# Multi-query attention beside a spectral filter: every fold of the first Fourier stage on VectorE, its constant as 128 rows, and a reordered end of the opening stage

## The chip, the cores and the metric

The kernel runs on one core of one Trainium2 chip. The metric is the device time in microseconds. Three runs of the kernel before the change took 697.56, 697.57 and 697.76 us; the median is 697.57 us. One more execution was profiled: it took 697.94 us, and its first to its last instruction span 696.1 us. All times inside the kernel below are microseconds from the start of that span.

## The reference

Two independent parts work on two inputs of 2048 rows by 448 columns, and their results are put side by side.

Part A is attention with 16 heads of width 28 that share one key and one value head:

```
q = (x @ wq) as 16 heads;  k = x @ wk;  v = x @ wv
p = softmax(q @ k.T * 28 ** -0.5)
a = concat(p @ v) @ wo
```

Part B is a global filter in the frequency domain:

```
X = rfft2(x);  X = X * (w_r + 1j * w_i);  b = irfft2(X)
```

All inputs and the result are float32.

## The kernel before

The kernel has an opening stage (up to about 97 us) and an attention stage (from there to the end).

In the opening stage the projections are computed and the forward transform of part B along the 448 columns and the first step along the 2048 rows are done. The projection x times wq runs in four chunks c of 512 rows and four groups g of four heads; each group holds a few spare rows in which k and v travel along. A float32 operand is split into a rounded high part and a rest (`split_w`, `split_x`), and one group of one chunk is eleven products (line 267) into one PSUM bank `pq`. ScalarE copies the bank to `qraw` (line 271, in `evac`) and VectorE takes the largest absolute value of it (line 272, `qmx`). The four groups of chunk 0 come first; the loop from line 310 then runs the twelve pairs (c, g) with c from 1 to 3, counted by n = 4(c-1)+g from 0 to 11.

The transform's first stage comes in eight portions q. For each portion, `fft1_load` brings a 512 KB block `xb` and a small table `fw` on SyncE's DMA queue, with four `xb` buffers in all. `fft1_fold` forms the sums and differences that the symmetry of the transform allows, into a tile `f` of two buffers, so that fold q+2 has to wait for the products that read fold q. `fft1_a` multiplies `f` by the constant `cs1` (64 products, line 120) and `fft1_b` multiplies the result by `fw` (16 products, line 132); then two stores per portion put the result into a DRAM tile `t1` (line 142). The tuple `slots` names the pairs n after which a portion's `fft1_a`, the load of portion q+4, the fold of portion q+2 and `fft1_b` of portion q-1 stand.

A fold is eight tensor-tensor operations: two of 113x512 at line 99 (one sum, one difference), two more of 113x512 at lines 102 and 103, and four of 113x256 at lines 104 to 107. Before the change the differences of lines 99 and 103 run on GpSimd (POOL), the rest on VectorE (DVE).

The keys and values are gathered out of the spare rows of `qraw` into the tile `kf` by small transfers (`fetch`, line 197): fourteen on SyncE's queue, seven on GpSimd's. `keys` splits the keys into `ka`. `kf` is first filled with a column of constants, `cvk`, by a GpSimd copy (line 291). 

At the end of the stage comes a bound on the scores. `qmx` is reduced to `qm`, multiplied to `prod` (line 355), a product with `blk` (line 357) gives `cvec`, four small products (line 363) and a reduction give one number `bits` (line 364). Each engine loads `bits` into a register (line 368) and branches (line 369): if the bound is too large, a slow path corrects the queries; the data here do not take it. `build_q(0, 0, True)` makes the first group's query tile `qa` with DVE and ScalarE copies; it stands before the computation of `bits`. After the branch the values are transposed by sixteen products (line 401) and copied to `vs` (line 402).

The attention stage has 256 half steps: two products `s` (line 649), an exponential on ScalarE (line 652) and, one step later, the products with the values (line 631). The second and third stages of the transform are put between these by a list written out in the code (`at`, `mid`).

TensorE's (PE) instructions run in the order of the program (line 181). For the other engines and the queues the framework's scheduler sets the order, by its own estimates; each engine then executes its list strictly in order, waiting on semaphores. SyncE's queue (SP) and GpSimd's issue their DMAs in order too, so that one that has to wait holds up those behind it. `behind` gives the scheduler an order of issue and adds no semaphore.

The PSUM pool `p1` has eight banks in the opening stage; the attention pools `ps_x`, `ps_s` and `ps_o` are opened after it has been closed.

Of the kernel before, what the change touches and what calls it, by code (L numbers as in the profile page):

```python
# [9 lines left out]
F32 = mybir.dt.float32  # L10
# [4 lines left out]
ALU = mybir.AluOpType  # L15
# [23 lines left out]
def kernel(ctx: ExitStack, tc: tile.TileContext, t: dict):  # L39
# [41 lines left out]
    def fft1_consts():  # L81
        fc["cs1"] = fp.tile([113, 4, 113], F32, name="cs1", tag="cs", bufs=1)
        nc.sync.dma_start(fc["cs1"], t["cs1"])
# [10 lines left out]
    def fft1_fold(q):  # L94
        x = xb[q][0][:113]
        f = ff[q] = fp.tile([113, 4, 4, 2, 32], F32, name="f", tag="wi")
        xv = x.rearrange("p k (j h m) -> p k j h m", h=2, m=32)
        for h, (eng, op) in enumerate(((nc.vector, ALU.add), (nc.gpsimd, ALU.subtract))):
            eng.tensor_tensor(f[:, :, :, h], xv[:, :, :, 0], xv[:, :, :, 1], op=op)
# [3 lines left out]
        nc.gpsimd.tensor_tensor(o2, y[:, 0::2], y[:, 1::2], op=ALU.subtract)  # L103
        nc.vector.tensor_tensor(y[:, 0], e2[:, 0], e2[:, 1], op=ALU.add)
        nc.vector.tensor_tensor(y[:, 1], e2[:, 0], e2[:, 1], op=ALU.subtract)
        nc.vector.tensor_tensor(y[:, 2], o2[:, 0], o2[:, 1], op=ALU.subtract)
        nc.vector.tensor_tensor(y[:, 3], o2[:, 0], o2[:, 1], op=ALU.add)
# [3 lines left out]
    def fft1_a(q):  # L111
        f, cs1 = ff.pop(q), fc["cs1"]
        for p in range(2):
            pa = ps1[0].tile([128, 2, DF], F32, name="pa", tag="p")
            for e in range(2):
                for k, (n, o0) in enumerate(((113, 0), (112, 113))):
                    for h in range(2):
                        for r in range(2):
                            r0 = 64 * h + 32 * r
                            mm(pa[r0:r0 + 32, e, o0:o0 + n], f[:, 2 * r + k, 2 * p + e, h], cs1[:, 2 * r + k, :n],  # L120
                               start=True, stop=True)
            a = at1[q, p] = fp.tile([128, 2, DF], F32, name="a", tag=("pwr", "pwi")[p])
            nc.scalar.activation(a, pa, AF.Copy)  # L123

    def fft1_b(q):
        w = xb[q][1]
        pb = [ps1[0].tile([128, 2, DF], F32, name="pbb", tag="p") for _ in range(2)]
        for p in range(2):
            a = at1.pop((q, p))
            for h in range(2):  # L130
                for e in range(2):
                    mm(pb[h][64 * e:64 * e + 64, p], w[64 * h:64 * h + 64, 2 * p + e], a[64 * h:64 * h + 64, e],
                       start=True, stop=True)
        bs = fp.tile([128, 2, 2, DF], F32, name="bs", tag="cst" if q < 6 else "b2")
        for h in range(2):
            if q < 7:
                nc.scalar.activation(bs[:, h], pb[h], AF.Copy)
            else:
                nc.vector.tensor_copy(bs[:, h], pb[h])
        for e in range(2):  # L140
            n0 = 16 * e + 2 * q
            nc.sync.dma_start(t1.rearrange("(l s) n f -> s l n f", l=2)[:, :, n0:n0 + 2], bs[64 * e:64 * e + 64])

    def fft2_consts():
        for n in ("g1", "g2"):
            g = fp.tile([128, 128], F32, name=n, tag="g", bufs=1)
            nc.sync.dma_start(g, t[n])
            h = fc[n + "h"] = fp.tile([128, 128], F32R, name=n + "h", bufs=1)
# [6 lines left out]
    def build_q(c, g, first=False):  # L155
# [10 lines left out]
        for u in range(2):  # L166
# [9 lines left out]
            if first:  # L176
                nc.vector.tensor_copy(q[64:128, 2 * u:2 * u + 2], q[0:64, 2 * u:2 * u + 2].bitcast(F32))
        if not first:
            nc.sync.dma_start(q[64:128].bitcast(F32), q[0:64].bitcast(F32))

    pe_order = tc.manual_schedule(engines={mybir.EngineType.PE})
    ctx.enter_context(pe_order)


    with tc.tile_pool(name="w1", bufs=1) as w1, tc.tile_pool(name="p1", bufs=8, space=PSUM) as p1:
        ps1[0] = p1
# [3 lines left out]
        kmb = w1.tile([128, 1], F32, name="kmb")  # L190
        qmx = w1.tile([128, NG, NC], F32, name="qmx")

        def fetch(ms, hs, eng=nc.sync):
# [19 lines left out]
        with tc.tile_pool(name="x1", bufs=2) as x1:  # L213
# [60 lines left out]

            slots = (3, 5, 6, 7, 8, 9, 10)
            xs = {}
# [7 lines left out]
            for j in range(NK):  # L284
# [4 lines left out]
                xr[1, j] = raw(t["xa"][1, :, j], nc.sync)  # L289
            cvk = const("cvk", [64, 1], nc.sync)  # L290
            nc.gpsimd.tensor_copy(kf, cvk.to_broadcast([64, S]))
            fft1_consts()
# [17 lines left out]
            for c in range(1, NC):  # L310
                for g in range(NG):
# [16 lines left out]
                    if c == 1 and g == 0:  # L328
                        fft1_fold(1)
                        fft2_consts()  # L330
                    if c == 2 and g == 3:
# [11 lines left out]
                    if c == 3 and g == 2:  # L343
# [4 lines left out]
                        nc.vector.tensor_copy(kmb, pb[:, 0:1])  # L348
            fetched = fetch(range(12, 14), slice(0, S), nc.gpsimd)

        fft1_b(6)
        fft1_a(7)

        nc.vector.tensor_reduce(qm[:, 2:4], qmx[:, 2:4], axis=AX.X, op=ALU.max)
        nc.vector.tensor_scalar(prod, qm, kmb, None, op0=ALU.mult)
        pb2 = p1.tile([128, 64], F32, name="pb2", tag="p")
        mm(pb2[:, 0:NG], blk, prod, start=True, stop=True)
        nc.vector.tensor_copy(cvec, pb2[:, 0:NG])
        build_q(0, 0, True)
        fft1_b(7)  # L360
        pb3 = p1.tile([128, 64], F32, name="pb3", tag="p")
        for g in range(NG):
            mm(pb3[0:1, 4 * g:4 * g + 4], cvec[:, g:g + 1], sel4, start=True, stop=True)
        nc.vector.tensor_reduce(bits, pb3[0:1, 0:16], axis=AX.X, op=ALU.max)
        keys(1, fetched)

# [31 lines left out]

        pv = p1.tile([128, 16, 32], F32, name="pv", tag="p")
        for b in range(16):  # L400
            nc.tensor.transpose(pv[:, b], kf[32:64, b * 128:(b + 1) * 128], ident[32:64, 32:64])
        nc.scalar.activation(vs, pv, AF.Copy)


    aux_pool[0] = ctx.enter_context(tc.tile_pool(name="ps_x", bufs=X_BUFS, space=PSUM))
    ps_s = ctx.enter_context(tc.tile_pool(name="ps_s", bufs=S_BUFS, space=PSUM))
    ps_o = ctx.enter_context(tc.tile_pool(name="ps_o", bufs=O_BUFS, space=PSUM))
    ap = ctx.enter_context(tc.tile_pool(name="ap", bufs=2))
# [288 lines left out]
def _constants():  # L697
    f = np.float32
    c = {}
    cvk = np.zeros((64, 1))  # L700
    cvk[28] = -1.0
    cvk[60:] = 1.0
    c["cvk"] = cvk
    sel = np.zeros((128, 2, 128))
# [103 lines left out]
```

## Time and profile before

| Measured | Value |
|---|---|
| median of three runs | 697.57 us |
| profiled execution, its own time | 697.94 us |
| its span | 696.1 us |
| PE busy | 669.7 us (96%) |
| ACT busy | 528.8 us (76%) |
| DVE busy | 318.4 us (46%) |
| POOL busy | 88.2 us (13%) |
| mean granted TensorE clock | 0.980 |
| from the first exponential (98.40) to the end | 597.7 us |

In the rows of the profile, PE is TensorE's products and PEld its weight loads, DVE is VectorE, ACT is ScalarE, POOL is GpSimd and SP is SyncE; a name with a q is the engine's instruction queue. L99 is line 99 of the kernel. A row of the chain of waits gives a start, a duration, and the engine or transfer that the end of the kernel depended on at that time. A row of a table by windows gives, after the window and its length, the busy time of PE, PEld, DVE, ACT and POOL, the granted TensorE clock (1.00 is full speed), the busy share of the sixteen DMA engines and the rate in GB/s. `f<-xb` means that the tile f is written from xb.

### The profile page before, as it was taken

The page shows a single profiled execution, that of the slowest core. Times are in us where ns is not written, and L with a number is a line of the kernel's source. Part 1 is how long each engine was busy: PE and PEld are TensorE (multiplying, and loading weights), DVE is VectorE, ACT ScalarE, POOL GpSimd, SP SyncE. Part 2 cuts the span into 40 slices and gives each one's busy share as a digit, 9 for nine tenths or more (in the row PEclk, how much of TensorE's full clock was granted, in tenths as well). Part 3 has the DMA queues.
Part 4 walks back from the last instruction along what each step waited for, and adds up shares of the span by engine and source line. Part 5 has one row for each costly group of instructions (what it writes and reads, how often), then busy time and mean ns, then how long its engine had stood idle before and what let it go on. Part 6 is the DMA issues. An engine that isn't in the chain of part 4 may idle for free.

```text
span 696.1 us, 11835 instructions
## 1 busy us (share of the span) xinstructions
PE 669.7 (96%) x4478; PEld 374.5 (54%) x4478; DVE 318.4 (46%) x749; ACT 528.8 (76%) x607; POOL 88.2 (13%) x120
## 2 busy tenths in 40 slices
PE   9598959999999999999999999999999999999997
PEld 7476634555555555555555555555555555555555
DVE  7677542765989590207361512036342502062513
ACT  5253458888888888888888888888888888888882
POOL 1356624111111000000010010000011100000110
PEclk9898969999999999999999999999999999999999
DMA  7736675455555123202041413030231311020001
GB/s 234 230 104 193 165 203 115 111 137 138 136 134 141 46 69 91 64 18 71 14 128 45 107 50 75 14 74 14 79 92 58 86 54 43 22 71 15 28 28 54
DMA packets 34237, 61.80 MB, mean 89 GB/s; under 512 B 6354, under 2 KB 22852, under 8 KB 33190
## 3 DMA queue, kind: packets, MB, share of 16 engines
q1 hardware_dynamic: 30882, 49.28, 25.9%
q0 software_dynamic: 2720, 10.82, 6.3%
q8 instruction: 36, 0.59, 0.4%
q10 hardware_dynamic: 576, 0.92, 0.3%
q14 instruction: 23, 0.19, 0.1%
HBM read 29.28 MB, written 14.75 MB: 63 GB/s over the span
## 4 chain that ended last, share of the span: by engine, by line
PE 87%; DMA 4%; DVE 3%; POOL 2%; ACT 2%; issue 1%; SPq 1%; ACTq 0%; DVEq 0%; POOLq 0%
PE s L649 37%; PE po L631 34%; PE pw L553 4%; PE py L515 2%; PE pz L501 2%; DMA xb<-xb 2%; ACT p L652 1%; PE pq L267 1%; PE pa L120 1%; POOL xb L103 1%; PE s L553 1%; DMA fi<-fi 1%; DVE xl L259 1%; DMA raw<-wq 1%; DMA kf<-qraw 1%
## 5 line engine op out<-in xcount | busy, mean ns | idle before, releaser
L652 ACT ACTIVATE p<-s 128x1024 f32<-128x1024 f32 x512 | 484.8, 1031 | 96.0 <-PE s L649 96.0
L649 PE MATMUL s<-qa,ka 128*128 128x512 f32 x1024 | 301.0, 416 | 1.8 <-ACT p L652 1.2
L649 PEld LDWEIGHTS s<-qa,ka 128*128 128x128 f32 x1024 | 178.7, 189 | 139.9 <-ACT p L652 114.0
L631 PE MATMUL po<-p,vs 128*32 128x512 f32 x2048 | 246.0, 598 | 0.0
L631 PEld LDWEIGHTS po<-p,vs 128*32 128x32 f32 x2048 | 53.5, 109 | 123.7 <-issue 118.3
L560 DVE COPY ya<-pw 128x448 f32<-128x448 f32 x12 | 7.5, 624 | 144.4 <-PE pw L553 126.9
L541 DVE RECIPROCAL r<-r 128x128 f32<-128x128 f32 x64 | 60.7, 949 | 1.2
L493 POOL DMA_DIRECT2D fi<-fi x8 | 4.6, 572 | 246.2 <-PE pz L501 239.2
L521 DVE TENSOR_TENSOR y<-py,m 128x226 f32<-128x226 f32 x16 | 6.3, 394 | 64.0 <-ACT m L519 64.0
L504 DVE COPY z<-pz 113x512 f32<-113x512 f32 (+1 forms) x16 | 11.1, 691 | 49.1 <-PE pz L501 49.0
L524 POOL TENSOR_TENSOR yo<-y 128x226 f32<-128x226 f32 x16 | 9.3, 583 | 188.3 <-issue 174.5
L120 PE MATMUL pa<-cs,f 113*32 113x112 f32 (+1 forms) x512 | 17.7, 292 | 10.2 <-issue 7.3
L267 PE MATMUL pq<-xh,wqh 128*128 128x512 f32 x64 | 26.5, 415 | 0.0
L448 DVE CAST bh<-b 128x450 fp32r<-128x450 f32 x16 | 7.4, 461 | 40.9 <-PE pu L422 30.5
L267 PE MATMUL pq<-xh,wql 128*128 128x512 f32 x64 | 25.5, 399 | 0.1
L120 PEld LDWEIGHTS pa<-cs,f 113*32 113x32 f32 x512 | 14.8, 124 | 14.1 <-issue 9.8
L123 ACT ACTIVATE a<-pa 128x450 f32<-128x450 f32 x16 | 8.8, 548 | 16.8 <-PE pa L120 16.8
L271 ACT ACTIVATE qraw<-pq 128x512 f32<-128x512 f32 x16 | 9.0, 597 | 15.3 <-PE pq L267 15.3
L440 POOL DMA_DIRECT2D wr<-wr x16 | 8.5, 533 | 92.9 <-DVE pwr L458 73.9
L639 DVE COPY osb<-po 128x512 f32<-128x512 f32 x15 | 10.3, 689 | 20.9 <-PE po L631 20.9
L540 DVE STREAM_SHUFFLE r<-osb 128x128 f32<-128x128 f32 x64 | 19.0, 297 | 0.1
L267 PE MATMUL pq<-xl,wqh 128*128 128x512 f32 x48 | 19.0, 396 | 0.0
(119 smaller groups left out, 609.7 us busy)
## 6 DMA issues: line engine op xcount, KB each, us to landing
qa<-qa SPq DMA_DIRECT2D x15, 512.0 KB, 4.5
raw<-xa SPq DMA_DIRECT2D x16, 256.0 KB, 3.1
xb<-xb SPq DMA_DIRECT2D x8, 512.0 KB, 4.7
qa<-qh SPq DMA_DIRECT2D x60, 64.0 KB, 2.0
qa<-ql SPq DMA_DIRECT2D x60, 64.0 KB, 2.0
ob<-yo SPq DMA_DIRECT2D x16, 226.0 KB, 2.3
t<-bs SPq DMA_DIRECT2D x16, 225.0 KB, 5.0
wr<-wr POOLq DMA_DIRECT2D x16, 225.0 KB, 4.7
```

What stands on the lines that cost most here:

```text
L120: mm(pa[r0:r0 + 32, e, o0:o0 + n], f[:, 2 * r + k, 2 * p + e, h], cs1[:, 2 * r + k, :n], start=True, stop=True)
L267: mm(pq, w[:, j, gs], x[:, j], start=(j == 0 and n == 0), stop=(j == 3 and n == 1))
L501: mm(pz[:w, j], c2["c", q][:, j, o0:o0 + w], c2["F", q][:, j], start=True, stop=True)
L504: nc.vector.tensor_copy(z[:w], pz[:w].rearrange("p j (r n) -> p r j n", r=2))
L515: mm(py[:, k], z[:w, r, js], cs3[:w, k], start=True, stop=True)
L540: nc.vector.stream_shuffle(r, o, [DH] * 32)
L541: nc.vector.reciprocal(r, r)
L553: mm(p, x[c][:, g, s], w[:, g], start=(g == 0 and n == 0), stop=(g == NG - 1 and n == 2))
L631: mm(po[c, g][32 * i:32 * i + 32], vs[:, kc], ps[i // 2][:, i % 2], start=(kc == 0), stop=(kc == 15))
L639: nc.vector.tensor_copy(o, po[c, g])
L649: last = mm(s[:, j], ka[:, kc * 128:(kc + 1) * 128], qa[c, g][:, 2 * u + j], start=True, stop=True)
L652: nc.scalar.activation(p, s, AF.Exp, scale=SCALE)
```

## The change

The change has these parts.

- In `fft1_fold` the two operations that ran on GpSimd run on VectorE; all eight are now there.
- The constant `cs1` is loaded as a tile of 128 rows, padded with zeros, in place of 113.
- `slots` loses n = 7. Six portions have their `fft1_a` in the loop, the last two come behind it, and `fft1_b` trails as before.
- Behind the loop the order is: `fft1_a(6)`, the product `prod`, `fft1_b(5)`, the product with `blk`, `fft1_a(7)`, the four small products and `bits`, `build_q`, `fft1_b(6)`, the transposes of the values and their copy, `fft1_b(7)`, the second half of the keys, and only then the branch.
- `p1` has six banks; `ps_x` and `ps_o` are opened before it and lend their banks to `fft1_b`. The tile `bs` of portions 4 and 5 takes another buffer.
- `kf` is cleared by a GpSimd memset and gets its five constant rows by two DMAs of GpSimd's queue; the DMA of `cvk` on SyncE's queue and the GpSimd copy go.
- The constants `g1` and `g2` of the second stage are loaded on GpSimd's queue, later in the program.

```diff
     def fft1_consts():
-        fc["cs1"] = fp.tile([113, 4, 113], F32, name="cs1", tag="cs", bufs=1)
+        fc["cs1"] = fp.tile([128, 4, 113], F32, name="cs1", tag="cs", bufs=1)
         nc.sync.dma_start(fc["cs1"], t["cs1"])
...
-        for h, (eng, op) in enumerate(((nc.vector, ALU.add), (nc.gpsimd, ALU.subtract))):
-            eng.tensor_tensor(f[:, :, :, h], xv[:, :, :, 0], xv[:, :, :, 1], op=op)
+        for h, op in enumerate((ALU.add, ALU.subtract)):
+            nc.vector.tensor_tensor(f[:, :, :, h], xv[:, :, :, 0], xv[:, :, :, 1], op=op)
...
-        nc.gpsimd.tensor_tensor(o2, y[:, 0::2], y[:, 1::2], op=ALU.subtract)
+        nc.vector.tensor_tensor(o2, y[:, 0::2], y[:, 1::2], op=ALU.subtract)
...
-        f, cs1 = ff.pop(q), fc["cs1"]
+        f, cs1 = ff.pop(q), fc["cs1"][:113]
...
-        pb = [ps1[0].tile([128, 2, DF], F32, name="pbb", tag="p") for _ in range(2)]
+        if q == 6:
+            pb = [ps1[0].tile([128, 2, DF], F32, name="pbb", tag="p") for _ in range(2)]
+        else:
+            pb = aux2("pbb"), ps_o.tile([128, 2, DF], F32, name="po")
...
-        bs = fp.tile([128, 2, 2, DF], F32, name="bs", tag="cst" if q < 6 else "b2")
+        bs = fp.tile([128, 2, 2, DF], F32, name="bs", tag=("cst", "cst", "wr", "b2")[q // 2])
...
-            nc.sync.dma_start(g, t[n])
+            nc.gpsimd.dma_start(g, t[n])
...
-    with tc.tile_pool(name="w1", bufs=1) as w1, tc.tile_pool(name="p1", bufs=8, space=PSUM) as p1:
+    ctx.enter_context(tc.manual_schedule(engines={mybir.EngineType.PE}))
+    ps_x = ctx.enter_context(tc.tile_pool(name="ps_x", bufs=X_BUFS, space=PSUM))
+    ps_o = ctx.enter_context(tc.tile_pool(name="ps_o", bufs=O_BUFS, space=PSUM))
+    aux_pool[0] = ps_x
+    with tc.tile_pool(name="w1", bufs=1) as w1, tc.tile_pool(name="p1", bufs=6, space=PSUM) as p1:
...
+        nc.gpsimd.memset(kf, 0.0)
+        nc.gpsimd.dma_start(kf[DH:DH + 1], t["krow"][0:1])
+        nc.gpsimd.dma_start(kf[32 + DH:64], t["krow"][1:5])
...
-            slots = (3, 5, 6, 7, 8, 9, 10)
+            slots = (3, 5, 6, 8, 9, 10)
...
-            cvk = const("cvk", [64, 1], nc.sync)
-            nc.gpsimd.tensor_copy(kf, cvk.to_broadcast([64, S]))
             fft1_consts()
...
-                        fft2_consts()
...
-            fetched = fetch(range(12, 14), slice(0, S), nc.gpsimd)
-
-        fft1_b(6)
-        fft1_a(7)
+            fetch(range(12, 14), slice(0, S), nc.gpsimd)
+
+        fft1_a(6)
 
         nc.vector.tensor_reduce(qm[:, 2:4], qmx[:, 2:4], axis=AX.X, op=ALU.max)
         nc.vector.tensor_scalar(prod, qm, kmb, None, op0=ALU.mult)
+        fft1_b(5)
         pb2 = p1.tile([128, 64], F32, name="pb2", tag="p")
         mm(pb2[:, 0:NG], blk, prod, start=True, stop=True)
         nc.vector.tensor_copy(cvec, pb2[:, 0:NG])
-        build_q(0, 0, True)
-        fft1_b(7)
+        fft1_a(7)
         pb3 = p1.tile([128, 64], F32, name="pb3", tag="p")
         for g in range(NG):
             mm(pb3[0:1, 4 * g:4 * g + 4], cvec[:, g:g + 1], sel4, start=True, stop=True)
         nc.vector.tensor_reduce(bits, pb3[0:1, 0:16], axis=AX.X, op=ALU.max)
-        keys(1, fetched)
+        built = build_q(0, 0, True)
+        fft1_b(6)
+
+        pv = p1.tile([128, 16, 32], F32, name="pv", tag="p")
+        for b in range(16):
+            nc.tensor.transpose(pv[:, b], kf[32:64, b * 128:(b + 1) * 128], ident[32:64, 32:64])
+        nc.scalar.activation(vs, pv, AF.Copy)
+        fft1_b(7)
+        keys(1, built)
...
-        pv = p1.tile([128, 16, 32], F32, name="pv", tag="p")
-        for b in range(16):
-            nc.tensor.transpose(pv[:, b], kf[32:64, b * 128:(b + 1) * 128], ident[32:64, 32:64])
-        nc.scalar.activation(vs, pv, AF.Copy)
...
+    fft2_consts()
     fft3_consts()
...
-    c["cs1"] = np.stack([np.cos(te), pad(np.cos(to)), -np.sin(te), pad(-np.sin(to))], 1)
+    c["cs1"] = np.zeros((128, 4, 113))
+    c["cs1"][:113] = np.stack([np.cos(te), pad(np.cos(to)), -np.sin(te), pad(-np.sin(to))], 1)
```

More of the change, by code (lines that the diff above doesn't have):

```diff
@@ L176, in build_q @@
             if first:
-                nc.vector.tensor_copy(q[64:128, 2 * u:2 * u + 2], q[0:64, 2 * u:2 * u + 2].bitcast(F32))
+                end = nc.vector.tensor_copy(q[64:128, 2 * u:2 * u + 2], q[0:64, 2 * u:2 * u + 2].bitcast(F32))
         if not first:
-            nc.sync.dma_start(q[64:128].bitcast(F32), q[0:64].bitcast(F32))
-    pe_order = tc.manual_schedule(engines={mybir.EngineType.PE})
-    ctx.enter_context(pe_order)
-    with tc.tile_pool(name="w1", bufs=1) as w1, tc.tile_pool(name="p1", bufs=8, space=PSUM) as p1:
+            end = nc.sync.dma_start(q[64:128].bitcast(F32), q[0:64].bitcast(F32))
+        return end
+    ctx.enter_context(tc.manual_schedule(engines={mybir.EngineType.PE}))
[3 more added lines that the diff above has]
+    with tc.tile_pool(name="w1", bufs=1) as w1, tc.tile_pool(name="p1", bufs=6, space=PSUM) as p1:
         ps1[0] = p1
@@ L396 @@
             build_q(0, 0, True)
-        pv = p1.tile([128, 16, 32], F32, name="pv", tag="p")
-        for b in range(16):
-            nc.tensor.transpose(pv[:, b], kf[32:64, b * 128:(b + 1) * 128], ident[32:64, 32:64])
-        nc.scalar.activation(vs, pv, AF.Copy)
-    aux_pool[0] = ctx.enter_context(tc.tile_pool(name="ps_x", bufs=X_BUFS, space=PSUM))
     ps_s = ctx.enter_context(tc.tile_pool(name="ps_s", bufs=S_BUFS, space=PSUM))
-    ps_o = ctx.enter_context(tc.tile_pool(name="ps_o", bufs=O_BUFS, space=PSUM))
     ap = ctx.enter_context(tc.tile_pool(name="ap", bufs=2))
@@ L699, in _constants @@
     c = {}
[L700 to L703, printed above, removed]
+    c["krow"] = np.ones((5, S))
+    c["krow"][0] = -1.0
     sel = np.zeros((128, 2, 128))
```

## The prediction

> **What bounds the kernel now.** I read the page first: PE is busy 96% of the span, so only stretches in which it isn't can give much. The table by windows finds them, and says that they lie before 98.4 us:
>
> ```profile
> 12.00:14.00 2.00, 2.00 (x11) 1.65 (x10) 2.00 (x4) 1.42 (x3) 0.92 (x1) 1.00 0.11 32
> ...
> 26.50:34.00 7.50, 0.22 (x3) 0.18 (x2) 7.44 (x10) 2.19 (x5) 5.11 (x3) 0.76 0.72 227
> ...
> 60.00:70.00 10.00, 8.36 (x91) 5.99 (x91) 7.29 (x15) 2.08 (x4) 6.08 (x5) 0.66 0.65 183
> ...
> 86.00:94.50 8.50, 0.00 (x0) 0.00 (x0) 6.87 (x13) 2.51 (x4) 3.78 (x7) 0.64 0.82 213
> ...
> 98.40:677.85 579.45, 578.30 (x3538) 306.55 (x3541) 244.69 (x620) 484.77 (x526) 43.32 (x74) 1.00 0.28 73
> ```
>
> PE stands still from 26.5 to 33.8, around 60, and from 85.5 to 94.5, and each time its granted clock falls (0.76, 0.66, 0.64). The attention stage is full. The chain of waits says what PE waited for:
>
> ```profile
> 10.34 13.03 DMA xb<-xb
> ...
> 28.41 1.63 DVE f L99
> ...
> 55.89 2.82 POOL xb L103
> 58.77 1.35 issue
> 60.12 1.48 DVE f L105
> 61.99 3.22 PE pa L120 x62
> ...
> 94.55 1.88 PE pv L401 x16
> ...
> 98.40 4.70 ACT p L652 x5
> ```
>
> The first two stops are folds: the first came late with its block `xb`, that of portion 4 hung on GpSimd (line 103). Two more views explain the lateness, the SyncE queue's waits and the rows by tile:
>
> ```profile
> SPq L91 <- DMA cs<-cs: 4.9, 1, 4.9
> ```
>
> ```profile
> L99 DVE TENSOR_TENSOR f<-xb x8: 672/692/1633, 23.4 to 71.9; 113x512 f32<-113x512 f32 x8
> L103 POOL TENSOR_TENSOR xb<-f x8: 1326/1784/2817, 29.5 to 75.1; 113x512 f32<-113x512 f32 x8
> ...
> L104 DVE TENSOR_TENSOR f<-xb x8: 410/426/1466, 33.3 to 76.9; 113x256 f32<-113x256 f32 x8
> ```
>
> The constant `cs`, issued at 9.82, held up the issue of the next table until 22.31. From 12 to 14 us the DMA share was 0.11, which is 1.8 of 16 engines, with `cs` and `xb` both under way: a small transfer runs on about one engine, and what was issued behind it, `xb` 0 (landed 23.36) and the inputs of chunk 2 (first used 24.48), ends with it. The other rows (min/median/max ns) say that a DVE fold operation takes 0.69 or 0.43 us, and up to 1.6 beside GpSimd's.
>
> **Part by part.**
>
> *The 128-row constant.* If it is spread over all engines, 231 KB at the 355 GB/s of the window from 10 to 12 us is 0.65 us in place of 12.5. `xb` 0, issued by 10.3, then lands with its median of 4.7 us at 15.0. Bounds: nothing gained (it lands at 23.4), or 8.4 us earlier. By the DMA row alone I take the second, since 0.11 is so near to one engine in sixteen. [...]
>
> *The folds on DVE.* DVE has nothing from 17.65 to 23.39. A fold costs it 3.9 us without GpSimd beside it: three starts 0.61 apart and one 0.71 (it needs the difference just before), 2.54 in all, and four of 0.336 (77.22 to 78.22 are three of them), 1.34. So fold 0 is ready at 21.6 at best, and even with fold 1 (3.9), two `qmx` (1.2) and chunk 2's `xl` (2.5) ahead of its last operation, at 29.2, where the row says 33.8. PE is free at 26.5. I take no stop. PE then never idles from 16.4 on and keeps the full clock.
>
> PE from 26.5, by its full-clock rows (`pa` 1.69, `pbb` 0.92, eleven `pq` 2.5, 2.73 behind another kind, `pb` 0.54): `fft1_a(0)` and n = 4, 5 take 6.9; then `a1 b0`, n = 6; `a2 b1`, n = 7, 8; `a3 b2`, n = 9; `a4 b3`, n = 10; `a5 b4`, `pb`, n = 11 take 29.7. The last `pq` ends at 63.1 instead of 81.26. Check: 36.6 plus the first stop (7.3) and its slow clock (1.95), the second stop (3.4) and its slow clock (2.65), plus the pair `a`, `b` that moves behind the loop (2.61), is 54.5; the trace has 54.8.
>
> Is DVE fast enough? From 17.65 it has 8 folds (31.2), 14 `qmx` (8.5), chunks 2 and 3 of `xl` (5.0), `kl` and small ones (1.7): 46.4 us, until 64.1; PE allows its last `qmx` at 63.75 to 64.35. It is full to 99%. Each fold has slack of its own, though: fold q+2 may start when `fft1_a(q)` ends and is wanted two portions later, 7.9 to 10.5 us, and fold 7 only at 66. Cover is thus 4 us or more per fold, if DVE's list has a fair order. Bounds: nothing, or one stop like that at 58.7, 3.4 and 2.65 of slow clock, 6.0. I take 2.0, the back half of one fold (0.61 and four times 0.336) still open when PE comes, since one wait of 1.6 us (`pa` for `f` L104) is the small row before. The buffers of `p1` cover: a portion takes three of six banks now, five of eight before. `bs` in `wr` delays only filter loads that are wanted some 45 us into the attention stage.
>
> *The end.* Let T be the end of the last `pq`. Before, T to the first exponential was 17.1 us: `cvec` at T+3.1, `build_q` with `bs` copies on DVE until T+11.5, `bits`, the branch (92.84 to 94.53 for PE, 1.7), `pv` 1.88, `vs` 0.65, two `s` 1.3. After: `a6` to T+1.7, `b5` to 2.6 (ACT and DVE have `prod` at 1.8), `pb2` to 3.0, `cvec` 3.3, `a7` to 4.7, `pb3` 5.05, `bits` 5.25. DVE then builds `qa`: 0.55, 0.46, 0.69, then copies beside ACT's four of 0.63, last ones to about T+10.5 (ACT also has 1.6 us of `bs` and `vs`). PE: `b6` to 6.0; `pv` needs the two transfers of `kf` issued at T+0.9 and 1.4, 5.8 us to landing, so 7.2 to 8.3 (sixteen transposes, at full clock at least half of 1.88); `b7` to 9.2; register and branch 1.7, 10.9; two `s`, 12.2. ACT comes through its branch at about 12.2 as well. Cover: `bits` lies under `a7` and `b6`, `vs` under `b7`. So 12.2 instead of 17.1. Bounds: 10 (a branch that costs half, as its `TENSOR_LOAD` of 0.49 would allow) and 14 (`kl` of 2.33 on GpSimd starts ahead of `qt`, which took 2.51 beside it at 84.41 and 0.55 alone). I take 12.2. [...]
>
> *The rest.* `kf` by memset (four times the 0.52 of `wql`) replaces a copy of 2.71 that fell beside DVE's 2.27 at 14.06: ahead of PE's need, nothing on the path, bounds -0.4 to +0.4 (64 KB twice of `g` may come among the first inputs, at 336 GB/s). SP loses `cvk` (0.57) and the two `g`, one of which held its queue for 5.3 us: what stood behind, `kf` and `xb` 4, comes earlier. On POOL's queue `g` and `krow` cost 0.55 each, with nothing behind them that is near its time. Second half of the keys: wanted at half step 16, 36 us into the stage. From first exponential to end I keep 597.7: same instructions, PE busy 99.8%.
>
> **The sum.** The first exponential comes at 63.1 + 2.0 + 12.2 = 77.3 instead of 98.4: 21.1 us less. The profiled execution had 697.94, so 676.8; the median of the runs is 0.4 lower, so I say 676.5.
>
> **The rivals.**
> 1. DVE is the bound: its list is full to 99%, and if dependent operations go by durations (0.69, 0.43) and not by starts, a fold is 4.4 and the list 50.5 us, 4 us over; with a second stop of 6.0 at a bad place, 10 more: 686.5. For it: DVE's 20.8 busy of 26 us from 34 to 60; against: those rows hold 1.5s beside GpSimd.
> 2. The end keeps its order, since the scheduler puts `build_q` ahead of `bits` on DVE, or ACT's copies ahead of `vs`: 4.9 us of the gain go, 681.4. For: nothing but the framework's freedom.
> 3. The padded constant does not help, or the early blocks are late for another reason: `fft1_a(0)` waits as before, 7.3 and 1.95 more, 685.7. For: the first 17 us already move 234 GB/s; against: 0.11.
> 4. The other side: DVE's long rows are its own and not GpSimd's doing. With the largest of each row in the fold (1.63 to 1.75 four times, 1.47, 1.48, 1.51, 0.42) one costs 11.6, eight cost 61 us more, and the time is about 737. It decides from a fold of 6.6 us, where the 21.1 are eaten (8 times 2.7). Against: the medians of the rows are the short ones, so half of the folds already go without it.
>
> **How the numbers follow.** My forecast has 0.55 (from 672.5, the end at 10 and no wait in the loop, to 681), rival 1 0.15, rival 2 0.10, rival 3 0.12, rival 4 0.05, anything else 0.03. The range 672.5 to 687 takes in the forecast, rivals 2 and 3 and most of 1. 0.2% (1.4 us) is about what a measurement of this kernel can tell from no change. Only rival 4 and half of the rest are not faster: faster 0.93, same 0.01, slower 0.06.
>
> **What would show it.** Right: `cs` landing some 3 us after its issue; `fft1_a(0)` at 26.5 with `pa` at the full clock; no PE idle over 2 us until T, at 63 to 65; DVE's 113x512 at 0.69 in all sixteen and more; `bits` ahead of `qt`; one wait at the branch; first exponential 75 to 79. Wrong: PE waits on DVE at two portions or more, POOL held by a filter load ahead of its `kf` transfers, or an attention stage that is not 597 to 599 long.

## The result and the profile after

The changed kernel takes 676.68 us (median of four runs, 675.99 to 679.11), against 697.57 us for the kernel before it. The ratio is 0.9708, with a 95% interval of 0.9683 to 0.9733. The profiled execution took 676.5 us and spans 674.7 us, where it was 697.94 and 696.1. The forecast was 676.5.

The sum therefore came out right. Three of its terms did not, and their errors cancelled. The stages in the two traces:

| us | before | after | forecast for after |
|---|---|---|---|
| last `pq` of pair n = 3 ends | 26.55 | 27.09 | 26.5 |
| `fft1_a(0)` starts | 33.83 | 27.02 | 26.5 |
| last `pq` ends (T) | 81.25 | 63.63 | 65.1 (63.1 + 2.0) |
| T to the first exponential | 17.15 | 13.76 | 12.2 |
| first exponential | 98.40 | 77.39 | 77.3 |
| first exponential to the end | 597.7 | 597.3 | 597.7 |

First the table by windows of the changed kernel:

```profile
12.00:14.00 2.00, 2.00 (x10) 1.66 (x9) 1.93 (x4) 2.00 (x4) 0.78 (x2) 1.00 0.73 213
17.00:26.50 9.50, 9.50 (x44) 7.86 (x43) 9.44 (x18) 4.74 (x9) 1.13 (x2) 1.00 0.91 323
26.50:34.00 7.50, 7.50 (x93) 5.82 (x95) 7.50 (x16) 4.37 (x8) 0.00 (x0) 1.00 0.63 188
34.00:60.00 26.00, 26.00 (x451) 20.02 (x455) 25.37 (x50) 13.65 (x25) 1.75 (x4) 1.00 0.57 164
60.00:70.00 10.00, 9.32 (x197) 7.12 (x189) 8.03 (x16) 4.41 (x9) 5.71 (x7) 1.00 0.53 101
70.00:78.00 8.00, 5.39 (x37) 4.02 (x38) 6.59 (x14) 5.14 (x9) 4.06 (x8) 0.57 0.67 195
```

The reader sees that both stops of the loop have gone: PE is busy for the whole of 17 to 60 us and its clock stays at 1.00. What is left of the trouble lies from 70 to 78 us, where PE does 5.39 us of work at a clock of 0.57. DVE is now nearly as full as PE: 9.44 of 9.5, 7.50 of 7.5 and 25.37 of 26 us.

The SyncE queue's wait for `cs`, and the rows by tile (min/median/max ns, then when the group starts and ends), answer the two views of the folds:

```profile
SPq L91 <- DMA cs<-cs: 0.3, 1, 0.3
```

```profile
L99 DVE TENSOR_TENSOR f<-xb x16: 672/683/693, 17.1 to 60.2; 113x512 f32<-113x512 f32 x16
L103 DVE TENSOR_TENSOR xb<-f x8: 673/685/784, 19.5 to 61.5; 113x512 f32<-113x512 f32 x8
L104 DVE TENSOR_TENSOR f<-xb x8: 401/420/426, 20.8 to 62.3; 113x256 f32<-113x256 f32 x8
```

The wait has shrunk from 4.9 to 0.3 us. The first fold starts at 17.1 instead of 23.4, and no operation of a fold takes the 1.5 and 1.6 us that the largest of VectorE's rows took before. The end of the stage is read from DVE's and PE's timelines (start, duration, line, what, and in brackets the idle time before it and what ended that):

```profile
64.30 0.69 DVE L282 TENSOR_REDUCE qmx<-qraw 128x1 f32<-128x512 f32 x1 [0.61 <-ACT qraw L281]
66.79 0.55 DVE L163 TENSOR_SCALAR qt<-qraw,mask,cvec 128x512 f32<-128x512 f32 x1
67.37 2.48 DVE L164 CAST qh<-qt 128x512 fp32r<-128x512 f32 x1
69.88 0.69 DVE L165 TENSOR_TENSOR ql<-qt,qh 128x512 fp32r<-128x512 f32 x1
...
71.25 0.15 DVE L370 TENSOR_REDUCE bits<-pb 1x1 f32<-1x16 f32 x1
...
73.79 0.69 DVE L180 CAST qa<-qa 64x1024 fp32r<-64x1024 f32 x1 [0.60 <-ACT qa L176]
74.59 0.63 DVE L142 COPY bs<-pbb 128x450 f32<-128x450 f32 x1
75.13 0.62 DVE L142 COPY bs<-po 128x450 f32<-128x450 f32 x1
76.00 0.55 DVE L163 TENSOR_SCALAR qt<-qraw,mask,cvec 128x512 f32<-128x512 f32 x1 [0.25 <-DVEq L383]
```

```profile
71.05 1.79 PE L376 MATMUL pv<-ident,kf 32*128 32x32 f32 x16 [1.73 <-issue]
...
76.11 6.76 PE L656 MATMUL s<-qa,ka 128*128 128x512 f32 x16 [1.56 <-DVEq L383]
```

The cast `qh` takes 2.48 us; the same cast of the next group, at 76.58, takes 0.43. `bits` comes behind `qt`, `qh`, `ql` and two copies. PE stands for 1.73 us ahead of the transposes `pv` and for 1.56 us at the branch (line 383). The profile names no releaser for the first stop; the last two transfers of `kf` were issued from 64.55 us on, and those of this time took 4.1 to 5.8 us to land, so I read it as the wait for `kf`. The second stop ends 0.36 us after DVE's last `bs` copy (until 75.75). Two chains reach those `bs` copies within 0.1 us of each other: DVE's own query copies until 74.48, and PE's `fft1_b(7)`, whose last product ends at 74.56.

### The profile page after: what moved, and what is told of

It is laid out like the page before. It is cut to its first block, busy times and chain, and to the rows that moved or that the text cites. A ratio compares the mean times of both kernels' runs of the same rounds, so it can differ in the third digit from the quotient of the medians.

```text
span 674.7 us, 11800 instructions
## 1 busy us (share of the span) xinstructions
PE 665.1 (99%) x4478; PEld 371.9 (55%) x4478; DVE 320.2 (47%) x765; ACT 529.2 (78%) x607; POOL 63.4 (9%) x108
## 3 DMA queue, kind: packets, MB, share of 16 engines
q1 hardware_dynamic: 30544, 49.18, 26.5%
## 4 chain that ended last, share of the span: by engine, by line
PE 86%; ACT 1%; DMA 1%; ACTq 0%; issue 0%; SPq 0%
PE s L656 38%; PE po L638 35%; PE pw L559 5%; PE py L521 2%; PE pz L507 2%; DMA ka<-ka 1%; PE s L559 1%; ACT p L659 1%; PE pu L429 1%; PE pu L427 1%; PE pc L428 0%; PE pc L429 0%; PE pu L428 0%; PE pc L427 0%; ACT yb L564 0%; PE s L694 0%
## 5 line engine op out<-in xcount | busy, mean ns | idle before, releaser
L277 PE MATMUL pq<-xh,wql 128*128 128x512 f32 x64 | 25.4, 396 | 0.1
L548 DVE TENSOR_TENSOR osb<-osb,r 128x128 f32<-128x128 f32 x64 | 18.4, 288 | 1.2
L559 PE MATMUL pw<-woh,ol 128*128 128x448 f32 x51 | 18.8, 368 | 0.0
L559 PE MATMUL pw<-woh,oh 128*128 128x448 f32 x51 | 18.7, 368 | 0.0
L559 PE MATMUL pw<-wol,oh 128*128 128x448 f32 x51 | 18.6, 364 | 0.0
```

The costliest lines, as they stand in the source:

```text
L277: mm(pq, w[:, j, gs], x[:, j], start=(j == 0 and n == 0), stop=(j == 3 and n == 1))
L548: nc.vector.tensor_tensor(o, o, r, op=ALU.mult)
L559: mm(p, x[c][:, g, s], w[:, g], start=(g == 0 and n == 0), stop=(g == NG - 1 and n == 2))
```

## The experiments: which part gives what

Three kernels add parts to the kernel before; they share their runs of it (median 697.10 us).

**Only the 128-row constant.**

```diff
-        fc["cs1"] = fp.tile([113, 4, 113], F32, name="cs1", tag="cs", bufs=1)
+        fc["cs1"] = fp.tile([128, 4, 113], F32, name="cs1", tag="cs", bufs=1)
...
-        f, cs1 = ff.pop(q), fc["cs1"]
+        f, cs1 = ff.pop(q), fc["cs1"][:113]
...
-    c["cs1"] = np.stack([np.cos(te), pad(np.cos(to)), -np.sin(te), pad(-np.sin(to))], 1)
+    c["cs1"] = np.zeros((128, 4, 113))
+    c["cs1"][:113] = np.stack([np.cos(te), pad(np.cos(to)), -np.sin(te), pad(-np.sin(to))], 1)
```

> The kernel before with only the 128-row constant; GpSimd keeps its half of the folds. Theory (the 113-row transfer held back the early inputs): the first block lands near 15 us, fold 0 takes about 5 us beside GpSimd's two 1.8 us operations and is ready before 26.5, so the first stop of PE (7.3) and its slow clock (1.95) go; the second stop, on GpSimd, stays: 697.6 - 9.2 = 688.4, DMA share from 12 to 14 us above 0.6 instead of 0.11. Rival (the early transfers are late for their bytes alone): nothing, 697.6.

Measured: 691.62 us (691.31 to 691.92), ratio 0.9919 (0.9903 to 0.9936), 5.5 us faster. T is 75.38, and T to the first exponential is 17.09, as before. The windows of this kernel:

```profile
12.00:14.00 2.00, 2.00 (x10) 1.68 (x9) 1.97 (x4) 1.89 (x4) 0.18 (x1) 1.00 0.85 214
...
26.50:34.00 7.50, 5.31 (x71) 3.92 (x70) 6.90 (x14) 2.21 (x4) 2.33 (x2) 0.78 0.47 155
```

The DMA share from 12 to 14 us goes from 0.11 to 0.85: the third rival, that the padding does nothing, falls. But PE still stands for 2.2 us of the window from 26.5 to 34, with its clock at 0.78, since half of each fold still hangs on GpSimd. That remainder, 2.2 us and the slow clock behind it, is of the size of the 3 us by which the gain misses the expected 688.4.

**Only the folds on VectorE.**

```diff
-        for h, (eng, op) in enumerate(((nc.vector, ALU.add), (nc.gpsimd, ALU.subtract))):
+        for h, op in enumerate((ALU.add, ALU.subtract)):
...
-        nc.gpsimd.tensor_tensor(o2, y[:, 0::2], y[:, 1::2], op=ALU.subtract)
+        nc.vector.tensor_tensor(o2, y[:, 0::2], y[:, 1::2], op=ALU.subtract)
```

> The kernel before with only the folds moved wholly to VectorE; the constant keeps 113 rows. Theory: fold 0 still starts at 23.4 with the late block and is ready between 27.3 and 31, so 3 to 6.5 us of the first stop and some of its slow clock go, and the second stop (6.0 with its slow clock) goes; VectorE's list of 46.4 us then starts 5.7 us late and sets the pace from 23.4, so the last projection ends near 70 instead of 81.3: 686.5, at best 684, at worst 690. Rival (VectorE becomes the bound with long operations of its own): 697.6 or more.

Measured: 688.52 us (688.24 to 688.87), ratio 0.9875 (0.9858 to 0.9891), 8.6 us faster and inside the expected interval. Its window with the constant under way shows the share of the unpadded transfer again:

```profile
12.00:14.00 2.00, 2.00 (x10) 1.65 (x10) 2.00 (x4) 1.48 (x3) 0.86 (x1) 1.00 0.08 14
```

The first fold starts at 23.9 here, as late as before. What the move to VectorE gains is time per fold, not the early start.

**Both.**

> The kernel before with both the 128-row constant and all folds on VectorE, and its old end. Theory: no stop of PE at all, the last projection ends at 26.5 + 36.6 + 2.6 = 65.7 instead of 81.3, the end of 17.1 us stays as it is: 682 (681 to 684). What is then left to the new order of the end and the loop is some 5 to 6 us. Rival (the two are two cures for one stop): no better than the better of the two alone, 686.

Measured: 682.74 us (682.64 to 683.25), ratio 0.9793 (0.9776 to 0.9809), 14.4 us faster, where the two parts alone give 5.5 and 8.6: they add up. T is 66.80, and T to the first exponential 17.10. The loop is full:

```profile
34.00:60.00 26.00, 26.00 (x453) 19.67 (x453) 25.77 (x51) 13.32 (x24) 6.60 (x10) 1.00 0.72 208
```

What remains to the changed kernel, 682.74 to 676.68, about 6 us, belongs to the other parts of the change together; they were not run one by one. In the traces half of it is the loop, which has one pair of `a` and `b` less (2.6 us of PE's work) and ends at 63.63 instead of 66.80, and half is the new order at the end, which has that pair more and still takes 3.3 us less.

Two kernels take parts out of the changed kernel (runs of the kernel before: 697.37 us).

**The constant with 113 rows again.**

```diff
-        fc["cs1"] = fp.tile([128, 4, 113], F32, name="cs1", tag="cs", bufs=1)
+        fc["cs1"] = fp.tile([113, 4, 113], F32, name="cs1", tag="cs", bufs=1)
```

> The changed kernel with the constant back at 113 rows. Theory: the first block lands at 23 again, VectorE idles from about 17 to 23, fold 0 is ready at 27.3 to 31, and VectorE's list, 5 to 6 us late, moves the end of the last projection by about as much: 676.5 + 5 = 681.5 (679.5 to 685). Rival (the folds on VectorE alone cure the first stop): 676.5 to 678.

Measured: 682.25 us (680.24 to 682.92), ratio 0.9787, which is 5.6 us more than the changed kernel and close to the 681.5 expected. From 17 to 26.5 us DVE has little to do, and is then behind for the whole loop:

```profile
17.00:26.50 9.50, 9.50 (x44) 7.86 (x43) 2.03 (x4) 2.15 (x5) 0.74 (x2) 1.00 0.74 228
```

Two folds' worth of DVE's time (9.44 against 2.03 us busy) is lost there, and T moves from 63.63 to 68.98, 5.35 us (1.1 of them because the pair n = 3 already ends later in this trace, at 28.22).

**The differences on GpSimd again.**

```diff
-        for h, op in enumerate((ALU.add, ALU.subtract)):
+        for h, (eng, op) in enumerate(((nc.vector, ALU.add), (nc.gpsimd, ALU.subtract))):
...
-        nc.vector.tensor_tensor(o2, y[:, 0::2], y[:, 1::2], op=ALU.subtract)
+        nc.gpsimd.tensor_tensor(o2, y[:, 0::2], y[:, 1::2], op=ALU.subtract)
```

> The changed kernel with the differences of the folds back on GpSimd. Theory (the folds' hand-overs between the two engines made the second stop): one stop of PE in the loop comes back, 3.4 and up to 2.65 of slow clock: 680 to 682.5. Rival (the early blocks and the free place after n = 7 give GpSimd time enough, 3.6 us of work for each portion against 5.3 to 8): 676.5 to 678.

Measured: 686.57 us (685.38 to 688.08), ratio 0.9848, 9.9 us more than the changed kernel. Both expectations miss it. T hardly moves (64.46): with the early start and with the pair `a7` behind the loop, the loop itself can carry the slow folds. The price is paid behind the loop, where PE waits for the last fold. A row of the waits (who waits, for whom: us in total, times, longest):

```profile
PE pa L120 <- DVE f L104: 8.9, 1, 8.9
```

T to the first exponential is 24.42 us in place of 13.76 (in an execution of 688.08 us, 1.5 above the median). VectorE, slowed by operations of up to 1.7 us beside GpSimd, reaches line 99 of fold 7 at 66.24, where it is 60.2 in the changed kernel. GpSimd's half follows at 67.06, and VectorE's next operation of the fold comes only at 73.70, behind query copies in VectorE's list; the last four start at 77.17. So it is not the long operations alone: once the fold is late, its rest stands behind the work of the end in an in-order list.

## The experiments: is VectorE the bound?

The prediction said two things that pull apart: VectorE's list is full to 99%, and each fold has 4 us or more of cover if the list has a fair order. To tell which of them counts, line 99's two operations are done twice, with the same values; nothing else in the source is changed. Two more operations at starts 0.61 apart are 1.22 us per fold, 9.8 us for eight.

```diff
-        for h, op in enumerate((ALU.add, ALU.subtract)):
+        for h, op in enumerate((ALU.add, ALU.subtract, ALU.add, ALU.subtract)):
+            h %= 2
```

> The changed kernel with the two operations of line 99 done twice in each fold: 1.2 us more VectorE work per fold, 9.8 us in all, same values. It asks how near VectorE is to being the bound. Theory A (its list is full to 99%, so each further microsecond is on the path): 8 to 9 us slower, 685. Theory B (each fold has a cover of its own of 2.4 to 5 us, which is read off the gaps between the end of a fold and the products that read it): within 1.5 us of the changed kernel, 678 at most.

Measured: 687.09 us (686.5 to 688.47), ratio 0.9859, 10.4 us more than the changed kernel, nearer to the first theory (8 to 9) than to the second. The window shows VectorE without a gap and PE no longer full:

```profile
34.00:60.00 26.00, 24.61 (x345) 17.45 (x335) 25.94 (x49) 11.95 (x22) 0.52 (x1) 1.00 0.54 146
```

T goes from 63.63 to 74.45, 10.8 us, but most of that does not come by way of a fold. PE waits for folds 1.7 us in all, and the last `fft1_a` of the loop starts 2.3 us later (60.10 for 57.77; 3.2 counted from the first). The long wait is for another operation:

```profile
PE pb L355 <- DVE qm L352: 4.9, 1, 4.9
```

`qm`, here the reduction for the keys, is a small operation. In the changed kernel the framework put it ahead of folds 6 and 7 on VectorE's list (at 54.69); here it stands behind fold 6 and three operations of fold 7 (at 68.33), though the values that it reads were there before. PE stands for it from 63.6 to 68.5, and the eleven products `pq` behind it take 5.0 us instead of 2.8, most of them 0.63 us each instead of 0.39. So the edit changed the order of VectorE's list too, and that the loss is so near to the 9.8 us added is in part chance. What the run does show: the folds had cover of their own, the list as a whole had none to match. Fold 7 ends at 71.20 instead of 63.68, and the `fft1_a(7)` that reads it started at 66.48 in the changed kernel, so by these rows about 5 us would be lost with a better order too (an estimate; it was not run).

In the changed kernel both engines are full at the same time. By these rows less work on one of them alone would not shorten the loop; that was not tried.

## The experiments: the end of the stage

The last term, T to the first exponential, took 13.76 instead of 12.2 us. The suspect was `kl` on GpSimd, the rest of the key split, which starts ahead of `qh` at 67.37; the cast ends 0.3 us behind it. From GpSimd's timeline:

```profile
67.06 2.50 POOL L218 TENSOR_TENSOR kl<-kf,ka 32x1024 fp32r<-32x1024 f32 x1
```

The runs of the kernel before that go with these kernels have a median of 697.37 us for the first two and 696.98 for the other three.

**The key split waits for the built queries.** A copy of one element of the finished `qa` stands ahead of it on GpSimd's list.

```diff
-                behind(nc.gpsimd.tensor_copy(ka[:32, hs], kf[:32, hs]), after)
+                gate = w1.tile([1, 1], F32, name="gate")
+                g0 = nc.gpsimd.tensor_copy(gate, qa[0, 0][64:65, 3, CW - 1:CW].bitcast(F32))
+                behind(nc.gpsimd.tensor_copy(ka[:32, hs], kf[:32, hs]), g0)
```

> The changed kernel; the second half of the keys on GpSimd starts only when the query tile is built, since a one-element copy of the tile stands ahead of it. So VectorE's rounding copy of the queries no longer waits for GpSimd (2.48 us, else 0.43). Theory (two paths end together: VectorE's at 74.48, and the transfers of the values, the transposes and the last products at 74.53): nothing gained, 676.5 within 0.7. Rival (the blocked copy is the path): 2.0 less, 674.5.

Measured: 678.0 us (677.02 to 679.55), ratio 0.9726, so no gain. Yet the suspect is confirmed: with GpSimd away the cast is short.

```profile
68.52 0.43 DVE L164 CAST qh<-qt 128x512 fp32r<-128x512 f32 x1
```

T to the first exponential is 11.53, 2.2 us less: for the end itself the rival held, and not the theory. But the attention stage is 601.4 instead of 597.3, 4.1 us more. In it stands a wait that the changed kernel does not have:

```profile
PE pu L429 <- DVE pwi L468: 2.3, 1, 2.3
```

Behind that wait sixteen products `po` (at 107.32) take 3.05 us, where those before and after them take 1.92. From 100 to 200 us PE is busy for 97.71 us at a granted clock of 0.98; in the changed kernel it is 100.00 us at 1.00.

**`fft1_b(7)` ahead of the transposes**, so that PE works while `kf` lands.

```diff
         fft1_b(6)
+        fft1_b(7)
 
         pv = p1.tile([128, 16, 32], F32, name="pv", tag="p")
...
         nc.scalar.activation(vs, pv, AF.Copy)
-        fft1_b(7)
```

> The changed kernel with the products of portion 7 ahead of the transposes of the values, so that they no longer stand behind the transfers that the transposes wait for. Theory (two paths): VectorE, held by GpSimd, still comes to the last copies at 74.5, nothing gained, 676.5 within 0.7. Rival (the transposes' wait is the path alone): the products end some 2 us earlier and so does everything behind them, 674.7.

Measured: 676.61 us (675.77 to 677.05), ratio 0.9709: no change, as expected, and T to the first exponential is 13.63. PE's stop has only moved, to line 135:

```profile
71.94 0.41 PE L135 MATMUL pbb<-a,fw 64*64 64x225 f32 x2 [2.16 <-ACT a L123]
```

The second copy of `a` stands on ScalarE behind a copy of `qa` that waited 2.47 us for `ql`, so for the same blocked cast.

**The first filter loads ahead of the key split.** `filt_load(0)` is the part of the second stage that loads `wr` and `wi`. On GpSimd's list it has to wait for a store of `bs` (7.16 us in the trace), since `bs` has lent the buffer of `wr`, and so holds the split back without a gate. The rest of the edit, not shown, puts these loads into that function and leaves them out where they stood.

```diff
-        keys(1, built)
+        keys(1, filt_load(0))
```

> The changed kernel with the first filter loads on GpSimd's queue issued ahead of the second half of the keys, and the key split behind them. The filter loads wait for a store until about 73 us, so the key split starts when VectorE has built the queries, and the filter loads are not late. Theory (the run with the one-element copy had an end 2.2 us shorter and lost 4 us later, to a late filter load): the end shrinks from 13.8 to 11.6 us after the last projection and the attention stage keeps its 597.3 us: 674.4, profiled first exponential near 75.2. Rival (the end is held by the transfers of the values, not by VectorE): 676.5.

Measured: 675.88 us (675.25 to 677.67, five runs), ratio 0.9688 (0.9668 to 0.9708), where 674.4 was expected. The cast takes 0.43 us here too, but T to the first exponential is 13.51, no better than in the changed kernel, as the rival says. VectorE now waits for PE, ahead of the `bs` copies:

```profile
75.26 0.63 DVE L142 COPY bs<-pbb 128x450 f32<-128x450 f32 x1 [1.62 <-PE po L135]
```

This is the second of the two chains: `kf` lands, PE does `pv` after 1.53 us of standing (1.45 us of work, where it was 1.15 with the gate), then `fft1_b(7)`. It ended together with the first, and taking away the first alone shows it. With the gate the first chain was gone too, and yet the end was 2.0 us shorter than here: there the last product of `fft1_b(7)` ended 8.9 us after T (at 73.70), here 10.4 (at 75.22). Of this 1.5 us, 0.4 is the later start of `pv` and 1.1 the slower products: from the start of `pv` to the end of the last product of `fft1_b(7)` it is 3.15 us here and 2.07 there, and most rows of `fft1_b(7)` take 0.58 us here and 0.36 there.

**Both of the last two.**

```diff
         fft1_b(6)
+        fft1_b(7)
...
-        keys(1, built)
+        keys(1, filt_load(0))
```

> The kernel of the run before this one, and the products of portion 7 ahead of the transposes of the values. With VectorE no longer held up, the copies of portion 7 still stand behind the query copies on VectorE, which wait for ScalarE: 674.4, the same within 0.5. Rival (the transposes' wait for the values' transfers has become the path): 1 to 1.7 less, 673.

Measured: 675.91 us (675.23 to 678.45, five runs), ratio 0.9696 (0.9671 to 0.9721). T to the first exponential is 11.04, the shortest of all: with both chains cut 2.7 us go, where the filter loads alone gave 0.25, the swap alone 0.13, and the gate, which met a faster second chain, 2.2. For the end the rival held, but neither whole time that was expected (674.4 or 673) came: the attention stage takes 599.8, and gives 2.5 us back. In PE's timeline and in the waits of the attention stage:

```profile
70.59 1.20 PE L384 MATMUL pv<-ident,kf 32*128 32x32 f32 x16 [0.85 <-DMA t<-bs]
73.19 5.35 PE L661 MATMUL s<-qa,ka 128*128 128x512 f32 x14 [1.41 <-DVEq L390]
```

```profile
PE pu L434 <- DVE pwi L471: 1.3, 1, 1.3
```

What gives the time back is not a late filter load, as I had thought of such a loss: the row names VectorE's product `pwi` as what PE waits for (PE's product `pc` waits 0.6 us more for it), and no engine waits for a filter load there. VectorE's list has the query split of a later group ahead of the first filter product, and that split waits for the transfers that read the tiles it writes. Its row in this kernel, and then in the changed kernel:

```profile
96.30 1.36 DVE L171 CAST qh<-qt 128x512 fp32r<-128x512 f32 x1 [3.49 <-DMA qa<-qh]
```

```profile
98.36 0.43 DVE L164 CAST qh<-qt 128x512 fp32r<-128x512 f32 x1 [0.63 <-DMA qa<-qh]
```

The first filter product starts 26.4 us after the first score product here (99.55 and 73.19), 25.4 in the changed kernel (101.48 and 76.11) and 27.6 with the gate (102.89 and 75.26). The order of these three is that of the attention stages, 599.8, 597.3 and 601.4. In the other three kernels of this section it starts 23.7 to 23.9 us after, and the stage takes 597.1 to 597.5 us: only a start later than the changed kernel's goes with a loss. One step further back, SyncE's queue holds some of those query transfers behind the first blocks `b` that are read back from `t1`:

```profile
SPq L181 <- DMA b<-t: 3.9, 2, 3.5
```

With the gate that wait is 3.0 us, and the changed kernel has none. But with the filter loads alone it is 5.2 us and the attention stage still takes 597.4, so it cannot be the whole cause; what makes the first filter product late was not settled, and no kernel was run that only moves the split or the blocks. Both last kernels have a median 0.8 us below the changed kernel's, but the intervals of the ratios overlap, so they are not shown to be faster.

**The values behind the branch again.**

```diff
-        pv = p1.tile([128, 16, 32], F32, name="pv", tag="p")
-        for b in range(16):
-            nc.tensor.transpose(pv[:, b], kf[32:64, b * 128:(b + 1) * 128], ident[32:64, 32:64])
-        nc.scalar.activation(vs, pv, AF.Copy)
         fft1_b(7)
         keys(1, built)
...
             build_q(0, 0, True)
 
+        pv = p1.tile([128, 16, 32], F32, name="pv", tag="p")
+        for b in range(16):
+            nc.tensor.transpose(pv[:, b], kf[32:64, b * 128:(b + 1) * 128], ident[32:64, 32:64])
+        nc.scalar.activation(vs, pv, AF.Copy)
```

The second `build_q` is the one inside the branch, so the transposes now stand behind it.

> The changed kernel with the transposes of the values and their copy behind the branch, as before the change. Theory (TensorE now waits at the branch for nothing but `bits`, and the transposes then stand on the path again): they run from about 74 us at the slow clock, 1.9 us and the copy behind them, and the first score product starts at 77.4 instead of 76.1: 678, from 677.5 to 679. Rival (TensorE waits for VectorE at that time anyway, so they lie beside it): 676.5.

Measured: 678.44 us (677.44 to 680.4), ratio 0.9729, 1.8 us more than the changed kernel and 0.4 from the 678 expected. T to the first exponential is 16.14. PE stands before the branch, and the transposes then run in front of everybody:

```profile
75.87 1.91 PE L410 MATMUL pv<-ident,kf 32*128 32x32 f32 x16 [3.31 <-DVEq L379]
```

## Why the prediction was right, and where it was not

*The 128-row constant: right.* The share went from 0.11 to 0.73 (0.85 with this part alone), and the first fold started at 17.07, behind other work of VectorE and with no wait for its block; the blocks `xb`, the first issued at 10.62, land after 3.6 us in the median, where `xb` 0 took 13.0 before. I had said 15.0 for its landing. (The table whose issue waited until 22.31 was that of portion 1, and not the next one; that of portion 0 had been issued at 13.55.) That 128 rows would be spread over all engines was my estimate, from a share near one in sixteen. With 113 rows the share was 0.11 at 32 GB/s (the kernel before) and 0.08 at 14 GB/s (the same with the folds moved). The 0.85 and 0.73 with 128 rows are of all transfers together: the constant no longer holds the others up (a wait of 0.3 us behind it instead of 4.9), but no view shows its own share. With 113 rows put back into the changed kernel the share there is 0.45, as other transfers run in that window, but the first fold still waits 7.1 us for its block.

*The folds on VectorE: right in the price, the cover half right.* Eight operations cost 0.68 and 0.42 us, and no PE stop is left before T. The 2.0 us taken for one fold's late back half did not come at all. This is the first term that was mis-sized: T came at 63.63, 1.5 us before the forecast, though the trace started 0.5 us later. That start, the end of n = 3, lies between 26.2 and 28.3 in the traces of the kernels here, with the order of the opening the same, and so is no part of the change. The 2.0 came out as 0 because the list just fits. "Cover is thus 4 us or more per fold, if DVE's list has a fair order" left out what else stands on that list. With 1.22 us more per fold PE waited 1.7 us in all for folds, but 4.9 us for `qm`, a small operation that stood behind them. Slack to a fold's own due time is not slack of a list in which every operation queues behind the others; "full to 99%" was the sentence to go by.

*The end: the mechanism right, the size 1.6 us short.* I took 12.2 and named 14 as the bound if `kl` starts ahead of the queries. It did, at 67.06. The block fell on `qh` and not on `qt`, and cost 2.05 us (2.48 for 0.43). The cast started 0.31 us after `kl` and ended at 69.85, 0.29 us after `kl` ended at 69.56. I had the row of `qt` that took 2.51 us beside `kl` before, and left it in the bounds. Had I put it in and nothing else, I would still have named only half of the cause, since the wait for `kf` ended at the same time: 13.51 and 13.63 with one of the two cut, 11.04 with both (the 11.53 of the gate had a second chain that was 1.5 us shorter).

"`bits` ahead of `qt`", given as what would show the step right, was wrong. The framework put it five operations later, at 71.25, the order of the second rival, and it cost nothing. The reason is another term that was wrong, 1.7 us for register and branch: here they lie under the work. Rows of the tile `bits`, and of line 383:

```profile
L382 DVEq TENSOR_LOAD <-bits x1: 541/541/541, 74.7 to 74.7; - x1
```

```profile
L383 DVEq COMPARE_BRANCH  x1: 72/72/72, 75.3 to 75.3; - x1
```

VectorE loads the register at 74.7 and branches at 75.3 while its last copy still runs until 75.75, and its next operation starts 0.25 us later. Before, the same branch cost it 1.38 us, as it had nothing left to do. So the second rival (681.4) was half true in its order and wrong in its price.

*The rest: nothing that can be seen.* The attention stage kept its length (597.3 for 597.7). The remark that the filter loads are wanted "some 45 us into the attention stage" was far too high: in the kernels here the first filter product, which reads them, comes 24 to 28 us after the first score product. It decided nothing in the changed kernel: no engine waits for a filter load there.

*The sum.* 2.0 too much in the loop, 0.5 for the start of the trace, 1.6 too little at the end: 77.39 against 77.3. The agreement to 0.1 us is luck; that to 2 us is not.

*The rivals.* The first, VectorE as the bound (686.5), did not come, but was near: with 1.22 us more per fold the kernel took 687.09, by a wait for VectorE, if not for a fold. The third (685.7) fell with the padding alone. The fourth, long rows that are VectorE's own, fell with the sixteen operations of line 99, the longest of which takes 0.693 us.

## What to carry to other kernels

- Behind a constant of 113 rows, at a DMA share of 0.11, the next block landed after 13.0 us; behind one of 128 rows the blocks took 3.6 in the median. Where a small transfer holds up others at such a share, try its number of rows before the order of the loads: 15 rows of zeros gave 5.5 us here.
- Work given to GpSimd was not free for VectorE: beside it VectorE's own operations took up to 1.6 us instead of 0.69, and two in-order lists stood in series (with the differences back on GpSimd, VectorE waited 5.9 us in all for line 103, and GpSimd 18.2 for line 99). Where VectorE can just take the work back, do so, then add a known amount of work to see whether it has become the bound. Look in that trace at what is waited for, and not at the total alone: the added work can change the order of the list.
- When a cut shows nothing, look for a second chain that ends at the same place, and cut both before giving up. And see what the earlier start brings forward: here the stage behind it gave back what the end gained.

## What the runs showed that was not expected

- PE's products were slow behind some of its short stops and not behind others, and in these traces the length of the stop alone does not decide. After 1.73 us of standing (the changed kernel) and 1.53 (the filter loads ahead of the split), the sixteen transposes took 1.79 and 1.45 us; after 1.16 (the gate) and 0.85 us (both of the last two) they took 1.15 and 1.20. In the changed kernel the granted clock is 1.00 up to 71.18 us and 0.50 from there to 81.42, and most rows of `fft1_b(7)` take 0.58 us, where those of `fft1_b(5)` take 0.36. Yet after 2.16 us of standing, with `fft1_b(7)` ahead of the transposes, its rows take 0.41 and 0.36 us and the transposes 1.18. What decides was not shown, and no run was made to test it.
- On VectorE the register load and the branch ran ahead of its last operations (0.25 us left of 1.38), so the late value cost little while the engine had other work.

Two things stay open. In the kernel with the filter loads ahead of the split, PE stood 1.53 us before the transposes, which took 1.45; with the gate it stood 1.16 and they took 1.15, and why their waits for `kf` differ was not found. And whether a version keeps both the 11.04 us of the end and the 597.3 us of the attention stage, which would be about 2.7 us less than the changed kernel, was not tried.
